# The entry to a backward attention loop, and three smaller edits, in a transformer block's training step

## The chip, the cores and the metric

One core of a Trainium2 chip. The time is device microseconds for one execution, the median of several; a profiled execution of the same kernel gives the trace. The engines are TensorE (PE; its weight loads PEld), VectorE (DVE), ScalarE (ACT), GpSimd (POOL) and SyncE (SP, which here only issues DMAs). DMAs are issued from SP's queue, and in the backward loop from ScalarE's too.

## The reference

A transformer block with adaptive layer norm, and its gradient. `x` is 2048 x 512 in bf16; attention has 32 heads of 16; the dense part has 1792 hidden units with a squared ReLU.

```python
mod = (silu(c) @ w_mod).reshape(...)              # sa, ca, ga, sb, cb, gb
h = layernorm(x) * (1 + ca) + sa
x = x + ga * attention(h, wqkv, wo)               # 32 heads, softmax over 2048 keys
h = layernorm(x) * (1 + cb) + sb
x = x + gb * (relu(h @ w1 + b1) ** 2 @ w2 + b2)
out, vjp = jax.vjp(f, x, wqkv, wo, w1, b1, w2, b2, c, w_mod);  grads = vjp(grad_out)
```

The outputs are the block's output and the gradients of all nine arguments.

## The kernel before

**Stages.** First a preparation (layer norm, q, k, v; L130 to L282). Then the forward attention (L625 to L653): 512 units, each a chunk of 512 queries (`qc`, 4), a group of 4 heads (`hg`, 8) and a tile of 128 keys (`kt`, 16). A unit makes scores (`fscore`), takes exps on ScalarE, and two units later multiplies by V (`fpv`). V carries a column of ones, so that row 16 of each head's result is the softmax denominator.

After the last key tile of a head group, VectorE copies the accumulator to `ostage` (L576), GpSimd casts it to `obf` (L578), SP copies four denominators to `rrows` (L581) and transposes `obf` into `O_un` (L582). After the last group of a chunk, `ffinish` (L586) transposes the denominators on TensorE (L591), inverts them and makes `O_c`. It runs when the loop has come to a unit number noted at L584, or in the loop's last pass. It also starts `dense_chunk` for those 512 tokens: a Python generator that the loop advances by one step per unit, 105 steps for chunks 0 to 2 with the pauses that it asks for. A dense chunk covers the output projection, the second layer norm, the up-projection (from `h2T`), its gradient, the down-projection and the gradient of the attention output (`attn_grad`, L495). The fourth dense chunk runs after the attention loop, in a tail (L743 to L755), interleaved with the weight gradients `dwa`; in it `act` is true, and some evictions go to ScalarE.

**The second layer norm's affine.** `xn2_c` is transposed by a DMA into `h2T` (L378), and four VectorE operations apply scale and shift per feature (L380), each over 128 partitions x 512. GpSimd makes the token-major `h2_c` at the same time (L383, L384).

**The entry to the backward loop (L772 to L956).** Two sets of tiles, `hsets`, hold k, v, q and dO of four heads at a time, each 128 x 2048 in bf16, with 16 rows of every 32 used and the rest filled with ones (k, v) or zeros (q, dO). GpSimd fills both sets first (L778). SP then loads set 0: `iqs` (token-major q), four DMAs each for k and q, the maxima `m_st` into a row of q, four for v (L792). Then follow `dOs_tok` (2 MB, one DMA, L797), `KS_tok` (2 MB, L800), the four loads of dO and one of its row `d_st` (L949, issued at L123), and `wT_pad` (2 MB of padded transposed weights, L956), which is read only in the last stage. GpSimd also fills a padding of KS_tok (L799) and two tiles `qz` (L803), and writes scaled q into `qz` (L850).

**The backward loop (L957 to L977).** 512 units again, four to a block, sixteen blocks to a head group. Step `j` is half a unit; a unit makes scores (L872), exps (L874), dP (L884) and dS on VectorE (L886). SP transposes dS by DMA, 512 KB per unit, into `dsT` (L892). TensorE adds to dK and dV (L900, L909), and, in steps 6 and 7 of the next block, to dQ from `dsT` and `KS_tok` (L927). `dsT` has two buffers, `dS_u` four.

**What sets the order.** In the forward loop the order of TensorE and ScalarE is as written, by `manual_schedule`; that of VectorE, GpSimd and SP comes from a planner that takes instructions as they become ready, by program order. In the backward loop the order of all but GpSimd is as written. A queue runs in order: a DMA that waits holds back those behind it. In the loop, DMAs for later heads are put at steps with `at(j, ...)`; `load` issues on ScalarE's queue. Loads of the next head begin at step 14 of each head (128 steps); stores of dK/dV and dQ go out at its end.

Of the kernel before, what the change touches and what calls it, by code (L numbers as in the profile page):

```python
# [14 lines left out]
AF = mybir.ActivationFunctionType  # L15
# [9 lines left out]
DH = 16  # L25
# [9 lines left out]
def kernel(  # L35
# [6 lines left out]
    n = A_x.shape[1]  # L42
    assert A_x.shape[2] == D and n % 512 == 0 and n <= 2048
    TT = n // P
    QC = n // 512
# [8 lines left out]
    DVE = nc.vector  # L54
    ACT = nc.scalar
    POOL = nc.gpsimd
    SP = nc.sync
# [13 lines left out]
    modcol = persist.tile([P, 6, DC], F32, name="modcol")  # L71
# [12 lines left out]
    dOs_st = dram.tile([P, TT, D], BF, name="dOs_st")  # L84
# [7 lines left out]
    dOT_st = dram.tile([D, n], BF, name="dOT_st")  # L92
    m_st = dram.tile([H, n], BF, name="m_st")
    d_st = dram.tile([H, n], BF, name="d_st")
    wpad_st = dram.tile([D, 16 * P], BF, name="wpad_st")
    wT_st = dram.tile([16, P, D], BF, name="wT_st")
# [17 lines left out]
    def row_loads(dst, srcT, hg, cols, aux=None):  # L114
        for h in range(4):
            i = hg * 4 + h
            yield dst[32 * h:32 * h + DH, :], srcT[i * DH:(i + 1) * DH, cols]
        if aux is not None:
            yield dst.rearrange("(h c) n -> c h n", h=4)[DH], aux[hg * 4:(hg + 1) * 4, cols]

    def load_rows(*args):
        for to, fro in row_loads(*args):
            SP.dma_start(out=to, in_=fro)  # L123
# [160 lines left out]
    with ExitStack() as ph:  # L284
# [16 lines left out]
        def flat(x):  # L301
            return x.rearrange("p a b -> p (a b)")
# [30 lines left out]
        def dense_chunk(c, O_c, act):  # L333
# [40 lines left out]
            for ti in range(4):  # L374
                t = 4 * c + ti
                DVE.tensor_scalar(xn2_c[:, ti, :], x1_c[:, ti, :], mv4[:, ti, 0:1], rstd2[:, t:t + 1], ALU.subtract, ALU.mult)
            h2T = cb.tile([P, 4, DC, P], BF, name="h2T", tag="T4")
            SP.dma_start(out=h2T.rearrange("p t o q -> p (t o) q"), in_=flat(xn2_c), transpose=True)  # L378
            for ic in range(DC):
                DVE.tensor_scalar(h2T[:, :, ic, :], h2T[:, :, ic, :],  # L380
                                  modcol[:, 4, ic:ic + 1], modcol[:, 3, ic:ic + 1], ALU.mult, ALU.add)
            h2_c = cb.tile([P, 4, D], BF, name="h2_c", tag="h2")
# [52 lines left out]
            for ti in range(4):  # L435
                t = 4 * c + ti
# [101 lines left out]
        fh, fe, fcur, fdone, dense = {}, {}, {}, [], []  # L538
# [21 lines left out]
        def fpv(u):  # L560
            qc, hg, kt = funits[u]
            if kt == 0:
                fcur["o"] = pools["o"].tile([P, 512], F32, name="oacc", tag="oacc")
                if hg == 0:
                    fcur["rr"] = ework.tile([H, 512], F32, name="rrows", tag="rrows", bufs=1)
                    fcur["ou"] = ework.tile([P, 4, HG, P], BF, name="O_un", tag="O_un", bufs=1)
            oacc = fcur["o"]
            ET = fe.pop(u)
            for hq in range(4):
                h = hg * 4 + hq  # L570
                lhsT = vaug[:, kt].rearrange("p h c -> p (h c)")[:, h * (DH + 1):h * (DH + 1) + 32]
                PE.matmul(oacc[32 * hq:32 * hq + 32, :], lhsT, ET[:, hq, :],  # L572
                          start=(kt == 0), stop=(kt == TT - 1), tile_position=(0, 32 * hq), skip_group_check=True)
            if kt == TT - 1:
                ostage = ework.tile([P, 512], F32, name="ostage", tag="ostage", bufs=1)
                DVE.tensor_copy(ostage[:], oacc[:])  # L576
                obf = ework.tile([P, 512], BF, name="obf", tag="obf", bufs=2)
                POOL.tensor_copy(obf[:], ostage[:])  # L578
                for hq in range(4):
                    h = hg * 4 + hq  # L580
                    SP.dma_start(out=fcur["rr"][h:h + 1, :], in_=ostage[32 * hq + 16:32 * hq + 17, :])  # L581
                SP.dma_start(out=fcur["ou"][:, :, hg, :], in_=obf[:], transpose=True)  # L582
                if hg == HG - 1:
                    fdone.append((u + 5, qc, fcur["rr"], fcur["ou"]))  # L584

        def ffinish(qc, rr, ou):  # L586
            O_c = cb.tile([P, 4, D], BF, name="O_c", tag="O_c")
            for ti in range(4):
                t = qc * 4 + ti
                pr = mm()  # L590
                PE.transpose(pr[:, 0:H], rr[0:H, ti * P:(ti + 1) * P], identf[0:H, 0:H])  # L591
                DVE.reciprocal(r_inv[:, t, :], pr[:, 0:H])
                DVE.tensor_tensor(O_c[:, ti, :].rearrange("p (g h d) -> p g h d", g=HG, h=4),
                                  ou[:, ti].rearrange("p g (h c) -> p g h c", h=4)[:, :, :, 0:DH],
                                  r_inv[:, t, :].rearrange("p (g h) -> p g h", g=HG).unsqueeze(3).to_broadcast([P, HG, 4, DH]),
                                  ALU.mult)
            SP.dma_start(out=o_st[:, qc * 4:(qc + 1) * 4, :], in_=O_c[:])
            dense.append(dense_chunk(qc, O_c, qc == QC - 1))
# [32 lines left out]
        with ExitStack() as ph2:  # L631
            pools["s"] = ph2.enter_context(tc.tile_pool(name="psS", bufs=3, space=bass.MemoryType.PSUM))
            pools["o"] = ph2.enter_context(tc.tile_pool(name="psO", bufs=1, space=bass.MemoryType.PSUM))
            pools["mm"] = ph2.enter_context(tc.tile_pool(name="psM", bufs=1, space=bass.MemoryType.PSUM))
            with tc.manual_schedule(engines={PE.engine, ACT.engine}):
                for u in range(NF + 6):
                    if u < NF:
                        if funits[u][2] == 4 and u + TT < NF:
                            fload(*funits[u + TT][0:2])
                        fscore(u)  # L640
                    if 2 <= u < NF + 2:
                        fpv(u - 2)
                    if u % 4 == 2 and u // 4 < 16:
                        later_stage(u // 4)
                    if dense and wait == 0:
                        wait = next(dense[0], -1)
                        if wait < 0:
                            dense.pop(0)
                            wait = 0
                    elif wait > 0:  # L650
                        wait -= 1
                    if not open_group[0] and fdone and (u - 2 >= fdone[0][0] or u == NF + 5):
                        ffinish(*fdone.pop(0)[1:])  # L653
# [118 lines left out]
    strm, hsets = [], []  # L772

    def head_set(i):
        strm.append(tc.alloc_tile_pool(name=f"phIs{i}", bufs=1, side="right"))
        hs = {key: strm[i].tile([P, n], BF, name=f"i{key}{i}") for key in ("k", "v", "q", "do")}
        for key in hs:
            POOL.memset(hs[key][:], 1.0 if key in ("k", "v") else 0.0)  # L778
        hs["qs"] = strm[i].tile([P, TT, 64], BF, name=f"iqs{i}")
        hsets.append(hs)  # L780

    def kvq_loads(hg):
        hs = hsets[hg % 2]
        yield hs["qs"][:], q_st[hg]
        yield from row_loads(hs["k"], qkT_st[1], hg, slice(0, n))
        yield from row_loads(hs["q"], qkT_st[0], hg, slice(0, n), m_st)
        yield from row_loads(hs["v"], vT_st, hg, slice(0, n))

    for i in range(2):
        head_set(i)  # L790
    for to, fro in kvq_loads(0):
        SP.dma_start(out=to, in_=fro)  # L792
    jpool = tc.alloc_tile_pool(name="jpool", bufs=1)
    wT_pad = jpool.tile([P, 16, D], BF, name="wT_pad")
    qpool = tc.alloc_tile_pool(name="qpool", bufs=1)
    dOs_tok = qpool.tile([P, TT, D], BF, name="dOs_tok")
    SP.dma_start(out=dOs_tok[:], in_=dOs_st[:])  # L797
    KS_tok = qpool.tile([P, TT, QPAD], BF, name="KS_tok")
    POOL.memset(KS_tok[:, :, D:QPAD], 0.0)  # L799
    SP.dma_start(out=KS_tok[:, :, 0:D], in_=k_st[:])  # L800
    qz = [qpool.tile([P, TT, 4, 32], BF, name=f"qz{i}") for i in range(2)]
    for i in range(2):
        POOL.memset(qz[i][:], 0.0)  # L803

# [10 lines left out]
    with ExitStack() as ph:  # L817
# [21 lines left out]
        def at(j, f, *args):  # L839
            todo.setdefault(j, []).append((f, args))  # L840
# [6 lines left out]

        def spread_qz(hg):
            st = hsets[hg % 2]
            POOL.tensor_scalar(qz[hg % 2][:, :, :, DH:2 * DH], st["qs"].rearrange("p t (h d) -> p t h d", h=4),  # L850
                               SCALE, None, ALU.mult)

        def plan_head(hg):
# [92 lines left out]
                    else:  # L946
                        at(cur["j"] + 6, load, dQtP[hg], st["dq"][:])

        load_rows(hsets[0]["do"], dOT_st, 0, slice(0, n), d_st)  # L949
        spread_qz(0)  # L950
        load_head(0)
        for hg in range(1, HG):
            plan_head(hg)
        for i, key in enumerate(("q", "k", "v", "do")):
            at((HG - 1) * 128 + 14 + 8 * i, load_grads, i // 2, (hsets[0]["q"], hsets[0]["k"]) if i < 2 else (hsets[0]["v"], hsets[0]["do"]), i % 2)
        SP.dma_start(out=wT_pad[:], in_=wT_st.rearrange("j p d -> p j d"))  # L956
        with tc.manual_schedule(engines={PE.engine, ACT.engine, DVE.engine, SP.engine}):  # L957
            for j in range(2 * NU + 10):
                u, pair, sub = j // 2, j % 2, j % 8
# [202 lines left out]
    if _rest_zero:  # L1162
        zt = persist.tile([P, 2048], BF, name="zeros2048")
        DVE.memset(zt[:], 0.0)
        for o in _rest_zero:
# [9 lines left out]
            while r0 < R:  # L1175
                rr = min(P, R - r0)
# [36 lines left out]
```

## Time and profile before

| | us |
|---|---|
| median of 3 runs | 2971.3 (2969.22 to 2974.01) |
| profiled execution | 2962.25 |
| its span | 2960.5 |
| forward attention loop, about | 186 to 1103 of the span |
| tail with the fourth dense chunk | 1103 to 1322 |
| entry to the backward loop (first fill to first dP matmul) | 1322.1 to 1347.6 |
| backward loop, first to last dQ eviction | 1367.9 to 2782.5 |

| engine | busy us | share |
|---|---|---|
| PE | 2502.8 | 85% |
| PEld | 728.6 | 25% |
| DVE | 1712.2 | 58% |
| ACT | 2185.0 | 74% |
| POOL | 444.1 | 15% |

The shares are means over stages with different limits, so a change is judged in its own stretch. The profile's queue names mean DMA issues (SPq, ACTq); a name such as `dsT<-dS_u` is destination and source. The granted TensorE clock has a mean of 0.80 of full speed.

### The profile page before, as it was taken

What the parts mean: (1) busy time and instruction counts of PE and PEld (TensorE: products, weight loads), DVE (VectorE), ACT (ScalarE), POOL (GpSimd) and SP (SyncE); (2) the same over time, 40 slices, a digit from 0 to 9 for tenths busy, and PEclk for the clock granted to TensorE, in tenths of its full rate; (3) what the DMA queues carried; (4) which work ended last, traced back from release to release, by engine and by line L of the source; (5) the groups of instructions that cost most, each with busy time, mean ns of one, the idle gap of its engine ahead of it and who ended that gap; (6) DMA issues with size and microseconds to landing.
All of it is one profiled execution on the core that took longest, in us unless ns stands there. A gap on an engine that the chain in (4) does not pass through costs nothing.

```text
span 2960.5 us, 45854 instructions
## 1 busy us (share of the span) xinstructions
PE 2502.8 (85%) x16942; PEld 728.6 (25%) x17006; DVE 1712.2 (58%) x2046; ACT 2185.0 (74%) x3432; POOL 444.1 (15%) x385
## 2 busy tenths in 40 slices
PE   6799988878888886987888888889898888888878
PEld 2111122212212222431222222222222222222323
DVE  6100044233413424526888888888888888878783
ACT  4699999989989981006777777778777777878521
POOL 3010012020311221211110101101010110101261
PEclk9555578768957878996889898888778888879989
DMA  9751144326344446739999999999999999999941
GB/s 254 199 131 41 28 104 118 93 69 140 96 103 105 134 111 174 163 107 237 198 208 200 197 209 199 208 196 205 202 199 208 203 205 198 202 209 201 202 117 43
DMA packets 1395889, 474.98 MB, mean 160 GB/s; under 512 B 1320321, under 2 KB 1369989, under 8 KB 1395281
## 3 DMA queue, kind: packets, MB, share of 16 engines
q1 hardware_dynamic: 1389088, 455.82, 78.1%
q10 hardware_dynamic: 6576, 16.23, 1.6%
q8 instruction: 134, 2.20, 0.3%
q14 instruction: 91, 0.74, 0.1%
HBM read 83.78 MB, written 61.10 MB: 49 GB/s over the span
## 4 chain that ended last, share of the span: by engine, by line
PE 27%; DMA 17%; ACT 7%; DVE 5%; issue 3%; SPq 1%; POOL 1%; DVEq 0%; ACTq 0%; POOLq 0%
DMA dsT<-dS_u 15%; PE psS_u L872 8%; ACT E_u L874 6%; PE dqacc L927 5%; PE accVK L909 4%; PE accVK L900 3%; DVE dS_u L886 2%; PE psS_x L872 2%; PE dwa L724 2%; PE psD_u L884 1%; PE pwq L1129 1%; PE dwa L733 1%; DMA out_dram<-dwres 1%; DVE prod L1106 0%; SPq L1023 0%
## 5 line engine op out<-in xcount | busy, mean ns | idle before, releaser
L886 DVE TENSOR_TENSOR dS_u<-psD_u,E_u 128x1024 bf16<-128x1024 f32 x1024 | 1190.9, 1217 | 258.3 <-PE psD_u L884 178.7
L874 ACT ACTIVATE E_u<-psS_u 128x512 bf16<-128x512 f32 x1536 | 866.0, 632 | 283.6 <-PE psD_u L884 256.2
L558 ACT ACTIVATE ET<-psST 128x1024 bf16<-128x1024 f32 x1024 | 947.1, 1235 | 40.9 <-PE psST L556 40.5
L872 PE MATMUL psS_u<-ik,iq 32*128 32x512 bf16 x1536 | 523.4, 438 | 20.7 <-DMA iq<-m_st 11.6
L556 PE MATMUL psST<-qt_sb,kt_sb 32*128 32x512 bf16 x2048 | 460.9, 508 | 87.3 <-ACT ET L558 36.7
L884 PE MATMUL psD_u<-iv,ido 32*128 32x512 bf16 x2048 | 453.6, 437 | 29.3 <-DMA ido<-d_st 13.1
L927 PE MATMUL dqacc<-dsT,KS_tok 128*32 128x512 bf16 x2048 | 212.7, 502 | 150.2 <-DMA dsT<-dS_u 113.5
L874 ACT ACTIVATE E_u<-psS_x 128x512 bf16<-128x512 f32 x512 | 332.5, 649 | 6.1 <-PE psD_u L884 4.4
L572 PE MATMUL oacc<-ET,vaug 128*32 128x512 bf16 x2048 | 271.5, 520 | 4.7 <-DVE ostage L576 4.1
L576 DVE COPY ostage<-oacc 128x512 f32<-128x512 f32 x32 | 22.0, 689 | 377.1 <-PE oacc L572 348.3
L900 PE MATMUL accVK<-dS_u,qz 128*32 128x512 bf16 x2048 | 228.0, 434 | 13.8 <-ACT vkb L912 13.0
L909 PE MATMUL accVK<-E_u,dOs_tok 128*16 128x512 bf16 x2048 | 228.8, 437 | 0.0
L942 POOL TENSOR_TENSOR dQacc<-dQacc,dqtmp 128x512 f32<-128x512 f32 x64 | 81.2, 1269 | 913.2 <-ACT dqtmp L937 913.2
L872 PE MATMUL psS_x<-ik,iq 32*128 32x512 bf16 x512 | 214.3, 419 | 0.6
L556 PEld LDWEIGHTS <-kt_sb 32*128 32x128 bf16 x2048 | 89.9, 96 | 461.1 <-issue 455.0
L872 PEld LDWEIGHTS <-iq 32*128 32x128 bf16 x2048 | 99.7, 93 | 375.9 <-issue 362.9
L884 PEld LDWEIGHTS <-ido 32*128 32x128 bf16 x2048 | 123.1, 93 | 230.9 <-issue 207.8
L736 ACT ACTIVATE dwres<-dwa 128x512 bf16<-128x512 f32 (+1 forms) x17 | 9.7, 572 | 140.8 <-PE dwa L733 71.8
L927 PEld LDWEIGHTS <-KS_tok 128*32 128x32 bf16 x2048 | 52.7, 106 | 210.3 <-issue 165.4
L572 PEld LDWEIGHTS <-vaug 128*32 128x32 bf16 x2048 | 56.0, 98 | 184.3 <-issue 184.3
L900 PEld LDWEIGHTS <-qz 128*32 128x32 bf16 x2048 | 56.1, 94 | 154.1 <-issue 153.8
L578 POOL CAST obf<-ostage 128x512 bf16<-128x512 f32 x32 | 20.6, 644 | 448.6 <-DVE ostage L576 428.8
(244 smaller groups left out, 2051.3 us busy)
## 6 DMA issues: line engine op xcount, KB each, us to landing
kt_sb<-qkT_st SPq DMA_DIRECT2D x128, 64.0 KB
dsT<-dS_u SPq DMA_TRANSPOSE x512
wA<-in_B_w_dram SPq DMA_DIRECT2D x4, 1792.0 KB
wB<-in_B_w_dram SPq DMA_DIRECT2D x4, 1792.0 KB
s_st<-tk SPq DMA_DIRECT2D x9, 512.0 KB
dz_st<-tk SPq DMA_DIRECT2D x9, 512.0 KB
slab<-s_st SPq DMA_DIRECT2D x9, 512.0 KB
slab<-dz_st SPq DMA_DIRECT2D x9, 512.0 KB
```

Source lines behind the costliest of these rows:

```text
L556: PE.matmul(ps[:, hi, :], kt_sb[r:r + 32, kt * P:(kt + 1) * P], qt_sb[r:r + 32, :], start=True, stop=True, tile_position=(r, 0))
L558: ACT.activation(ET[:, 2 * pair:2 * pair + 2, :], ps[:], AF.Exp, scale=SCALE)
L572: PE.matmul(oacc[32 * hq:32 * hq + 32, :], lhsT, ET[:, hq, :], start=(kt == 0), stop=(kt == TT - 1), tile_position=(0, 32 * hq), skip_grou ...
L724: PE.matmul(acc[:, 0:w], lhsT, rhs, start=(t == 0), stop=False)
L872: PE.matmul(psS[:], st["q"][r:r + 32, qt * P:(qt + 1) * P], st["k"][r:r + 32, kc * 512:kc * 512 + 512], start=True, stop=True, tile_positi ...
L874: ACT.activation(bst[u][0][:, hq, :], psS[:], AF.Exp, scale=SCALE)
L884: PE.matmul(psD[:, hi, :], st["do"][r:r + 32, qt * P:(qt + 1) * P], st["v"][r:r + 32, kc * 512:kc * 512 + 512], start=True, stop=True, til ...
L886: DVE.tensor_tensor(dS_u[:, 2 * pair:2 * pair + 2, :], psD[:], E_u[:, 2 * pair:2 * pair + 2, :], ALU.mult)
L900: PE.matmul(cur["vk"][32 * hq:32 * hq + 32, :], hst[hg]["qz"][:, qt, hq, :], bst[u][1][:, hq, :], start=(qt == 0), stop=False, tile_positi ...
L909: PE.matmul(acc[32 * hq:32 * hq + DH, :], dOs_tok[:, qt, (hg * 4 + hq) * DH:(hg * 4 + hq + 1) * DH], E_u[:, hq, :], start=False, stop=(qt ...
L927: PE.matmul(acc[32 * hq:32 * hq + 32, :], KS_tok[:, kc * 4 + kt, h * DH:h * DH + 32], tT[:, :, hq * 4 + kt, :], start=(kt == 0), stop=(kt ...
L942: POOL.tensor_tensor(dst2, dst, tmp[:], ALU.add)
```

## The change

There are five edits.

1. A forward chunk ends ten units after its last accumulation is evicted instead of five (`fdone`).
2. In the fourth dense chunk, ScalarE applies the affine to feature tiles 0 and 2 of h2T, VectorE to 1 and 3.
3. At the entry, VectorE fills tile set 0 and `qz[0]` and writes the first scaled q; GpSimd keeps set 1 (now filled last), the padding and `qz[1]`.
4. SP loads dO right after k, q and v; `dOs_tok` comes in four DMAs behind it.
5. The load of `wT_pad` leaves the entry and is issued from ScalarE's queue at step 400 of the loop's 1034.

```diff
             for ic in range(DC):
+                if act and ic % 2 == 0:
+                    ACT.activation(h2T[:, :, ic, :], h2T[:, :, ic, :], AF.Identity,
+                                   bias=modcol[:, 3, ic:ic + 1], scale=modcol[:, 4, ic:ic + 1])
+                    continue
                 DVE.tensor_scalar(h2T[:, :, ic, :], h2T[:, :, ic, :],
...
-                    fdone.append((u + 5, qc, fcur["rr"], fcur["ou"]))
+                    fdone.append((u + 10, qc, fcur["rr"], fcur["ou"]))
...
-            POOL.memset(hs[key][:], 1.0 if key in ("k", "v") else 0.0)
+            (DVE if i == 0 else POOL).memset(hs[key][:], 1.0 if key in ("k", "v") else 0.0)
...
-    for i in range(2):
-        head_set(i)
+    head_set(0)
     for to, fro in kvq_loads(0):
         SP.dma_start(out=to, in_=fro)
+    load_rows(hsets[0]["do"], dOT_st, 0, slice(0, n), d_st)
...
-    SP.dma_start(out=dOs_tok[:], in_=dOs_st[:])
+    for g in range(QC):
+        SP.dma_start(out=dOs_tok[:, 4 * g:4 * g + 4, :], in_=dOs_st[:, 4 * g:4 * g + 4, :])
...
-    for i in range(2):
-        POOL.memset(qz[i][:], 0.0)
+    DVE.memset(qz[0][:], 0.0)
+    POOL.memset(qz[1][:], 0.0)
+    head_set(1)
...
-            POOL.tensor_scalar(qz[hg % 2][:, :, :, DH:2 * DH], st["qs"].rearrange("p t (h d) -> p t h d", h=4),
+            (DVE if hg == 0 else POOL).tensor_scalar(qz[hg % 2][:, :, :, DH:2 * DH], st["qs"].rearrange("p t (h d) -> p t h d", h=4),
                                SCALE, None, ALU.mult)
...
-        load_rows(hsets[0]["do"], dOT_st, 0, slice(0, n), d_st)
         spread_qz(0)
...
-        SP.dma_start(out=wT_pad[:], in_=wT_st.rearrange("j p d -> p j d"))
+        at(400, load, wT_pad[:], wT_st.rearrange("j p d -> p j d"))
```

## The prediction

> **What bounds the kernel now.** The page's 40 slices come first: ScalarE at 9 or 8 tenths in the forward attention (slices 3 to 15), the DMA engines at 9 throughout the backward loop (slices 19 to 38). The change touches the ends of forward chunks, one step of the tail between the two loops, the entry to the backward loop, and the middle of that loop. Each needs its own stretch of the trace.
>
> Forward chunk ends, from the timeline (start us, length us, engine, line, operation, and in brackets the idle time ahead of it with what ended it):
>
> ```profile
> 356.21 1.02 ACT L558 ACTIVATE ET<-psST 128x1024 bf16<-128x1024 f32 x1 [1.98 <-PE psST L556]
> ...
> 598.61 0.34 SPq L348 DMA_DIRECT2D gf_st<-gf_c  x1
> ...
> 604.38 2.46 SPq L581 DMA_DIRECT2D rrows<-ostage  x4
> ...
> 608.06 0.28 PE L591 MATMUL pm<-identf,rrows 32*128 32x32 f32 x1 [5.44 <-DMA rrows<-ostage]
> ...
> 612.33 1.94 ACT L558 ACTIVATE ET<-psST 128x1024 bf16<-128x1024 f32 x2 [8.18 <-PE psST L556]
> ...
> 863.64 0.28 PE L591 MATMUL pm<-identf,rrows 32*128 32x32 f32 x1 [5.71 <-DMA rrows<-ostage]
> ...
> 868.07 2.85 ACT L558 ACTIVATE ET<-psST 128x1024 bf16<-128x1024 f32 x3 [8.59 <-PE psST L556]
> ```
>
> TensorE's order is written out by hand, so while the transposes of L591 wait for the denominators `rrows`, no scores are made and ScalarE starves. At the first chunk end the rows are there in time (1.98 us of ScalarE idle). At the second and third, SP is caught ahead of them in the `gf_st` store of the next dense chunk, which waits 8.2 us for GpSimd's gf_c.
>
> The entry, from the chain of waits:
>
> ```profile
> 1322.50 1.10 DMA rows_st<-racc
> ...
> 1334.38 1.75 POOL ido L778
> 1336.13 0.25 POOL KS_tok L799
> 1336.38 1.76 POOL qz L803
> 1338.14 1.35 SPq L123
> ...
> 1340.92 6.62 DMA ido<-d_st
> ...
> 1347.63 0.62 PE psD_u L884 x4
> ```
>
> The dO loads leave SP at 1338 to 1341 and the first dP matmul starts at 1347.63, though q and k were there at 1331.34. Beside it, DMA by half microseconds: the 4.2 MB of dOs_tok and KS_tok flow from 1333.75 to about 1344.7 (10.95 us, some 383 GB/s), dO until 1347.5, wT_pad (2.1 MB) from 1346.5 to 1352.3 (5.8 us). The first block's transposes get the DMA only then; its last one is issued at 1358.58 and the first dQ matmul goes at 1364.89: 12.4 us after the bulk has gone. So this entry ends with DMA work, not with the dP matmul. This reading decides the size of the gain.
>
> The loop, from the waits of TensorE between 1400 and 2700 us (total, times, longest):
>
> ```profile
> PE dqacc L927 <- DMA dsT<-dS_u: 109.2, 65, 5.8
> ```
>
> and from windows around the end of the third head (busy us per engine, granted clock, DMA share, GB/s):
>
> ```profile
> 1886.00:1896.00 10.00, 9.37 (x87) 2.96 (x84) 9.03 (x9) 9.72 (x20) 1.27 (x1) 1.00 1.14 220
> 1896.00:1902.00 6.00, 1.10 (x12) 0.28 (x12) 2.06 (x2) 0.00 (x0) 1.30 (x1) 0.55 1.10 265
> 1902.00:1916.00 14.00, 13.73 (x104) 2.93 (x100) 10.77 (x9) 10.87 (x21) 1.47 (x1) 0.50 1.14 193
> ```
>
> About half the blocks of four units wait for their transposes. DMA moves some 204 GB/s all the time, at which four transposes (2.1 MB) take 10.3 of a block's 11.1 us. Where a head ends, 1 MB of stores and a 256 KB load join in: all engines but DMA stop, and by the starts of the dQ evictions that block takes 15.5 to 16.1 us instead of 11 (mid heads). So 1.25 MB more DMA costs 4.5 us, with 0.5 us regained in the next block.
>
> **What the Trainium skill says.** "DMA: Bandwidth & Descriptors", section "Issuing engines are not separate DMA queues": DMAs issued by different engines run on the same 16 engines and interleave. The trace agrees: ScalarE's stores at a head's end hold back SP's transposes (5.37 us of TensorE idle at 1900.90). "VectorE: DVE Perf Modes", "Zero memsets can be issued as uint32": a memset takes a cycle per element whatever the type; a zero fill can be halved. The trace has VectorE fills of 165 ns for 128 bf16 and 70 ns for 14 f32, hence 0.83 ns per element and an estimated 1.76 us for 2048; that page's cycle at 0.96 GHz would give 2.13 us. "SBUF — State Buffer", "Who interferes with whom": VectorE in its two-port modes and GpSimd lock each other out. It fits h2T: 1.22 us each in the tail beside GpSimd's 4 us h2_c, where xn_c in the same shape takes 0.41.
>
> **The parts.** Baseline is the profiled execution: span 2960.5, time 2962.25.
>
> *Chunk end at u+10.* The two row copies before and at that chunk end lie 30.4 us apart for 16 units, so five units are 9.5 us, and the finish moves from 602.6 (608.06 less the 5.44 waited) to 612.1; rows landing at 608 would be in time. What is left is the first chunk's 1.98 us: (8.18 - 1.98) + (8.59 - 1.98) = 12.8 us. ScalarE is busy 875 of the 917 us between 186 and 1103, so its idle time is the forward's time. The whole dense chunk moves with it: 105 steps from unit 13 of the next chunk end at 118 of 128, so there is room. Its g_c load (589.28) moves behind the copies of the row (data ready at 594.25), so the `gf_st` wait should no longer block them. -12.8 us; between 0, if SP's backlog moves along, and -14. The last chunk finishes where it did (the loop's last pass), but GpSimd's 4.06 us gf_c, now 1091.68, slides to about 1102 and before the last obf cast (1103.74): +1.5, between 0 and +4.
>
> *h2T shared.* Four VectorE operations of 1.22 us stand between the transpose and the up-projection (4.64 us from 1144.75). Two go to ScalarE, where the row of that shape (xn, 128x512 from SBUF) takes 0.806 us: 1.6 beside VectorE's 2.4. ScalarE has nothing else there (12.06 us idle before 1150.46). -2.1, or 0 at the worst.
>
> *Entry.* Fills of set 0 on VectorE start behind its last row copy (1322.5), not at 1322.09: at 1.76 us the q fill ends at 1327.8, against 1327.39 now. VectorE's fills are thus no faster; set 1, KS padding and qz1 only leave the line. SP then issues at 0.42 us each: q and m to 1330.1, v to 1332.1, dO to 1333.8, d 1334.3, dOs_tok in four 1335.9, KS_tok 1336.5. d lands 2 us later, the first dP goes at about 1336.5: 11 us earlier. But the bulk starts flowing at 1336.5 instead of 1333.75 and, with wT_pad out of the way, ends at 1336.5 + 10.95 = 1347.4 instead of 1352.3. The transposes sit behind it in SP's queue (KS_tok is needed anyway): first dQ matmul at 1347.4 + 12.4 = 1359.8 instead of 1364.9. **-5 us**, between -2 (fills of 2.13 us and a slow dOs_tok in pieces) and -9 (zero fills halved, transposes overlapping). qz0's fill and scaling on VectorE, bounded by twice 0.41 and 2.8 us, are done by about 1334 to 1336, before K's first use at 1340; without that cover at most 2 us.
>
> *wT_pad at step 400.* 2.1 MB in a stretch bound by DMA, two steps after a head end. Alone it took 5.8 us; the head-end rate (4.5 per 1.25 MB) would make 7.5. The block at 1904 to 1916 has some 1.5 us of empty DMA to give. I take +5, between +1.5 and +9. Issue on ScalarE's queue is 0.4 us. If that queue backs up, the k load of step 403 and all exps behind it wait, as SP's dO load stood 6.6 us behind 4 MB; they would mostly stand in the same stall.
>
> Sum: -12.8 + 1.5 - 2.1 - 5 + 5 = **-13.4 us**, 2948.9 in the profiled execution. The median of the runs is 2971.3, 9 us above that execution, so 2957.9; I say 2958.
>
> **Rivals.** *A (0.56)* is the above, 2951 to 2965 on its own. *B (0.17):* the forward stall moves along. For: SP's order is planned from program order and readiness, and the backlog is made by the dense chunk, which shifts by the same five units. Against: g_c falls behind the row copies. Then -0.6: about 2971. *C (0.15):* the loop has cover for wT_pad (1.5 of it paid) and the entry gains 6: -12.8 + 1.5 - 2.1 - 6 + 1.5 = -17.9, 2953. For: half the blocks don't wait for transposes. Against: the head ends. *D (0.12), slower:* at both inner chunk ends SP keeps its order, with the next head's q rows behind the dense chunk's dOT, delta and row stores. Now that row load is issued at 588.67 and already costs TensorE 1.8 us at 590.51; 10 us later it stalls the scores 10 us at each of two ends, +20: 2978. It decides from about 7 us per end upward (13.4 / 2). Against: in the new program order the load (unit 244) comes before the last of those stores (245), where before it came after.
>
> **How the numbers follow.** 0.2% is 5.9 us, about what measurement can tell. Faster (below 2965.4): 0.49 of A, 0.15 of C, 0.02 of B. Same: 0.06 of A, 0.13 of B, 0.04 of D. Slower: 0.11, mostly D. The range runs from C with the entry's best value, 2946, over B with noise to 2976, just short of D.
>
> **What would show it.** Right: no `rrows` wait at L591 in the second and third chunk end and ScalarE idle of about 2 us there; first dP near 1347.6 - 11 and first dQ only 5 us earlier, each after subtracting what the forward gave; DMA full from the bulk through the first block; one block near step 400 longer by some 5 us. Wrong: waits of psST for `qt_sb` at chunk starts (D), the `rrows` wait still there (B), or a first dQ earlier by 9 us or more, which would say that DMA was not what the entry ended with.

## The result, and the profile after

The kernel became slower. The kernel after takes 2981.66 us (median of 4 runs, 2979.35 to 2990.39), the kernel before 2970.27 (4 runs, 2969.22 to 2974.01) in the same comparison: a ratio of 1.0041, 95% interval 1.0019 to 1.0064. I had predicted 2958.0, with a range of 2946 to 2976. The profiled execution of after has a span of 2978.4 us, 17.9 more than the one of before.

A table of moments on the time axis shows where the difference arises. Each is the start of one instruction, in us from the start of the span.

| moment | before | after | difference |
|---|---|---|---|
| last accumulator of the second chunk copied | 593.6 | 592.2 | -1.4 |
| of the third chunk | 848.9 | 844.5 | -4.4 |
| of the last chunk | 1103.0 | 1095.6 | -7.4 |
| transpose of the last denominators (L591, L595 after) | 1110.6 | 1116.9 | +6.3 |
| first affine of h2T in the tail | 1144.8 | 1152.4 | +7.6 |
| first `racc` copy, ahead of the entry | 1320.0 | 1329.2 | +9.2 |
| first dP matmul | 1347.6 | 1345.6 | -2.0 |
| first dQ eviction | 1367.9 | 1372.4 | +4.5 |
| last dQ eviction | 2782.5 | 2798.4 | +15.9 |
| end of the span | 2960.5 | 2978.4 | +17.9 |

The forward loop did gain (7.4 us of the 12.8 that I had summed), and then lost it and more in one wait at its end. The entry gained 4.7 from the `racc` copies to the first dQ, and the loop lost 11.4.

The forward chunk ends, from the timeline of after (start us, length us, engine, line, operation, in brackets the idle time ahead of it and what ended it):

```profile
602.65 2.45 SPq L585 DMA_DIRECT2D rrows<-ostage  x4
604.83 4.06 POOL L346 TENSOR_TENSOR gf_c<-g_c,modbc 128x2048 bf16<-128x2048 bf16 x1
608.85 3.61 POOL L308 TENSOR_TENSOR racc<-racc,g_c 128x512 f32<-128x512 f32 x3
612.41 0.61 POOL L582 CAST obf<-ostage 128x512 bf16<-128x512 f32 x1
613.05 1.27 SPq L586 DMA_TRANSPOSE O_un<-obf  x1
616.62 0.31 PE L595 MATMUL pm<-identf,rrows 32*128 32x32 f32 x1 [5.20 <-DVE r_inv L596]
618.45 7.44 ACT L562 ACTIVATE ET<-psST 128x1024 bf16<-128x1024 f32 x8 [6.49 <-PE psST L560]
...
871.06 7.44 ACT L562 ACTIVATE ET<-psST 128x1024 bf16<-128x1024 f32 x8 [6.83 <-PE psST L560]
...
1080.30 3.83 SPq L521 DMA_TRANSPOSE dOT<-dOs_c  x3
...
1090.58 6.33 SPq L323 DMA_TRANSPOSE wB<-in_B_w_dram  x5
1096.96 0.58 SPq L338 DMA_DIRECT2D g_c<-in_grad_out_dram  x1
1102.46 4.05 POOL L346 TENSOR_TENSOR gf_c<-g_c,modbc 128x2048 bf16<-128x2048 bf16 x1
1106.54 2.06 SPq L350 DMA_TRANSPOSE gfT<-gf_c  x1
1109.62 2.84 SPq L585 DMA_DIRECT2D rrows<-ostage  x4
1110.02 0.61 POOL L582 CAST obf<-ostage 128x512 bf16<-128x512 f32 x1
1116.88 0.28 PE L595 MATMUL pm<-identf,rrows 32*128 32x32 f32 x1 [21.37 <-DMA rrows<-ostage]
```

Read it in two parts. At the second and third chunk end the denominators now come in time (`rrows` at 602.65), as predicted. But the third of the second end's four transposes waits 5.20 us for VectorE's `r_inv`. VectorE is in order, and ahead of it stands the first piece of `O_c`, which waits for `O_un`, whose cast to `obf` stands on GpSimd behind gf_c and three `racc` adds until 612.41, though its data were copied by about 592.9. ScalarE's idle time falls from 8.18 and 8.59 us to 6.49 and 6.83, not to 2.

At the last end SP has the transpose of gf_c ahead of the last four denominators. It was so in before too, as its timeline shows:

```profile
1085.96 0.58 SPq L338 DMA_DIRECT2D g_c<-in_grad_out_dram  x1
...
1091.68 4.06 POOL L346 TENSOR_TENSOR gf_c<-g_c,modbc 128x2048 bf16<-128x2048 bf16 x1
...
1098.34 2.03 SPq L350 DMA_TRANSPOSE gfT<-gf_c  x1
...
1103.70 2.58 SPq L581 DMA_DIRECT2D rrows<-ostage  x4
...
1110.60 0.28 PE L591 MATMUL pm<-identf,rrows 32*128 32x32 f32 x1 [7.71 <-DMA O_un<-obf]
```

There, gf_c was ready at 1095.7, some 7 us before the last accumulator was copied (1103.0), so the transpose was out of the way. In after, SP's order is another one. In before, g_c left at 1085.96, and behind it came the last `dOT` transpose of the third dense chunk, the stores of that chunk's attention gradient, and the denominators and `O_un` of the seventh head group. In after all of these stand ahead of g_c, some 10 us of issues, with the last five transposes of w1 behind them. The third dense chunk itself comes only 1.5 us later on the time axis (its first `dOT` transpose starts at 1070.59 against 1069.12), since the loop is ahead by most of what five units take.

So g_c leaves SP at 1096.96, and gf_c is ready only at 1106.5. SP issues nothing between 1098.1 and 1106.54: it waits for gf_c with the transpose `gfT`, and the denominators, ready since about 1096.3, stand behind it and leave at 1109.62. The wait grows from 7.71 to 21.37 us.

The entry, from the chain of waits of after (start, length, what):

```profile
1331.72 1.11 DMA rows_st<-racc
...
1334.21 0.56 DVE iv L782
...
1336.14 0.92 DVE iq L782
...
1343.25 2.25 DMA ido<-d_st
...
1345.59 0.62 PE psD_u L890 x4
...
1348.69 10.86 DMA dsT<-dS_u
```

The fills are 1.76 us for ones and 0.91 for zeros, dO follows v at once, and the dP matmuls wait for nothing else. The last line is the first transpose of dS, which stands behind the bulk of the loads; the next dS waits for it until 1359.6, and the first dQ matmul follows at 1369.4.

The loop, from the waits of TensorE between 1400 and 2700 us (total, times, longest), and from windows around the end of the third head (busy us of PE, PEld, DVE, ACT and POOL, granted clock, DMA share, GB/s):

```profile
PE dqacc L933 <- DMA dsT<-dS_u: 114.2, 65, 7.4
```

```profile
1897.00:1904.00 7.00, 6.79 (x56) 2.08 (x52) 6.27 (x7) 7.00 (x15) 1.27 (x1) 1.00 1.16 214
1904.00:1916.00 12.00, 7.09 (x56) 1.60 (x56) 6.88 (x6) 5.36 (x11) 2.77 (x1) 0.57 1.05 218
1916.00:1926.00 10.00, 3.22 (x28) 0.90 (x24) 4.80 (x5) 3.88 (x8) 0.00 (x0) 0.78 1.17 274
```

The third window is the new one: TensorE has 3.2 us of work in ten, and the longest wait for `dsT`, 7.4 us, ends at 1926.6. This block, from the 49th dQ eviction to the next, took 17.8 us where before took 11.5. I call it block 49.

### The profile page after: what moved, and what is told of

Same layout as the page of the kernel before. It is cut to its first block, busy times and chain, and to the rows that moved or that the text cites. A ratio compares the mean times of both kernels' runs of the same rounds, so it can differ in the third digit from the quotient of the medians.

```text
span 2978.4 us, 45926 instructions
## 1 busy us (share of the span) xinstructions
PE 2510.4 (84%) x17006; PEld 729.0 (24%) x17006; DVE 1722.6 (58%) x2050; ACT 2184.4 (73%) x3434; POOL 433.1 (15%) x379
## 4 chain that ended last, share of the span: by engine, by line
PE 23%; DMA 17%; ACT 6%; DVE 5%; issue 3%; POOL 0%; SPq 0%; ACTq 0%; DVEq 0%; POOLq 0%
DMA dsT<-dS_u 16%; PE psS_u L878 7%; ACT E_u L880 6%; PE dqacc L933 5%; PE accVK L915 3%; PE accVK L906 3%; DVE dS_u L892 2%; PE psS_x L878 2%; PE pwq L1134 1%; PE psD_u L890 1%; DVE prod L1111 1%; DVE c12a L1119 0%; ACT vkb L918 0%; DVE tqa L1121 0%; DVE dxn L1108 0%
## 5 line engine op out<-in xcount | busy, mean ns | idle before, releaser
L429 DVE SCALAR_TENSOR_TENSOR rT<-pm,rT 128x512 bf16<-128x512 f32 x56 | 38.7, 692 | 114.2 <-PE pm L426 114.2
```

The costliest lines, as they stand in the source:

```text
L429: DVE.scalar_tensor_tensor(out=dzT[:, fc, :], in0=pds[:], scalar=2.0, in1=rT[:, fc, :], op0=ALU.mult, op1=ALU.mult, accum_out=db1p[:])
```

## The experiments with the kernel's own data movement

Theory Q says that the loss comes from the order of SP's queue at the end of the forward loop. Theory W says that the load of `wT_pad` in the loop costs some 6 us. The first four kernels ran as one group with the kernel before (2968.02 us there, 41 runs). Ratios are to before.

**Chunk ends back at u+5, everything else as in after.**

```diff
-                    fdone.append((u + 10, qc, fcur["rr"], fcur["ou"]))
+                    fdone.append((u + 5, qc, fcur["rr"], fcur["ou"]))
```

> The changed kernel with only the chunk end put back to five units; edits 2 to 5 stay. Theory Q (the loss sits at the end of the forward loop, where the last denominators stand behind the transpose of gf_c in SP's queue): the last chunk's first L591-type transpose comes 6 us earlier than in the changed kernel, its wait shrinks from 21.4 to about 8 us, and the time falls by about 6 us to 2975, still 4 to 5 above before. Theory W (the loss is the wT_pad load in a loop bound by DMA, with what follows from it): the time stays at 2979 to 2982.

2971.27 us (13 runs), ratio 1.0009 (0.9999 to 1.0018). The timeline of this kernel at the last end:

```profile
1110.25 0.28 PE L595 MATMUL pm<-identf,rrows 32*128 32x32 f32 x1 [8.12 <-DMA O_un<-obf]
```

The wait is back at 8.12 us, at the moment where before has it, and SP issues g_c at 1085.37 again, in before's order. So the edit of `fdone` makes the wait, and most of the loss. Block 49 is 6.8 us longer, against 4.2 gained at the entry in this profile. Without `u + 10` the other edits come to +3.3 us, which the interval doesn't tell from nothing.

**The edit of the chunk ends alone, in the kernel before.**

```diff
-                    fdone.append((u + 5, qc, fcur["rr"], fcur["ou"]))
+                    fdone.append((u + 10, qc, fcur["rr"], fcur["ou"]))
```

> The kernel before with only the chunk end at ten units. Theory Q: the inner chunk ends give 7.4 us, the last end takes 13.7, so about +6: 2976, with a wait of about 21 us for rrows ahead of the last chunk's transposes. Theory W: the forward's gain is all there is, -7 us: 2963.

2973.37 us (21 runs), ratio 1.0018 (1.0009 to 1.0026). From its timeline:

```profile
1118.26 0.28 PE L591 MATMUL pm<-identf,rrows 32*128 32x32 f32 x1 [21.78 <-DMA rrows<-ostage]
```

The same wait, in a kernel that has nothing else of the change, and the same late g_c (1098.10): 6.4 us ahead at the last accumulator, 7.7 behind at this transpose. The edit that I valued at -11.3 is worth about +5 by itself.

**u+10 at the first two chunk ends, u+5 at the third.**

```diff
-                    fdone.append((u + 10, qc, fcur["rr"], fcur["ou"]))
+                    fdone.append((u + (10 if qc < QC - 2 else 5), qc, fcur["rr"], fcur["ou"]))
```

> The changed kernel, but the chunk end at ten units only for the first two chunks and at five for the third, so that the third dense chunk is not late at the end of the forward loop. Theory Q: the inner gain of about 7 us stays and the last wait is back at about 8 us: 13 us less than the changed kernel, 2968, 2 us faster than before. Theory W: 2979 to 2982 as the changed kernel.

2975.86 us (13 runs), ratio 1.0028 (1.0018 to 1.0037), where theory Q expected 2968: a miss. The last wait did go back (8.01 us), but the third end became worse than in either kernel. Its timeline there:

```profile
858.75 4.04 POOL L346 TENSOR_TENSOR gf_c<-g_c,modbc 128x2048 bf16<-128x2048 bf16 x1
...
861.53 0.28 PE L595 MATMUL pm<-identf,rrows 32*128 32x32 f32 x1 [7.26 <-DMA rrows<-ostage]
...
866.30 0.61 POOL L582 CAST obf<-ostage 128x512 bf16<-128x512 f32 x1
...
870.54 0.31 PE L595 MATMUL pm<-identf,rrows 32*128 32x32 f32 x1 [7.97 <-DVE r_inv L596]
...
872.38 14.77 ACT L562 ACTIVATE ET<-psST 128x1024 bf16<-128x1024 f32 x16 [16.56 <-PE psST L560]
```

The finish came five units earlier, while the dense chunk ahead of it kept its later place, and SP issued g_c only at 853.40. So both the denominators (7.26) and the cast behind gf_c (7.97) were late, and ScalarE idled 16.56 us. The chunk end and the queues of SP and GpSimd have to fit each other; a shift of one alone moves the stall.

**`wT_pad` at the entry again, on SP behind `KS_tok`.**

```diff
-        at(400, load, wT_pad[:], wT_st.rearrange("j p d -> p j d"))
+        SP.dma_start(out=wT_pad[:], in_=wT_st.rearrange("j p d -> p j d"))
```

> The changed kernel with wT_pad loaded at the entry again, behind KS_tok on SP's queue. If the entry ends with DMA work, as the prediction read it: the block near step 400 loses its 6 us, but the first dQ eviction comes about 6 us later, so the time moves by less than 2 us: 2980 to 2983; the first dP stays 11 us earlier than before. Rival, that the entry ends with the first dP: the entry keeps its gain and the time falls by 6 us or more, to 2976 or less. Theory W: 2970 to 2976.

2981.18 us (5 runs), ratio 1.0049 (1.0036 to 1.0061), the same as after. Against the `racc` copies the first dP is 11.3 us earlier than in before, and the first dQ 1.1 later, where after has it 4.7 earlier. The load costs 5.8 us at the entry and 6.3 in the loop. Both readings hold: the entry ends with DMA work, and moving the load saves nothing.

## The experiments with plain DMAs

If Q is right, the u+10 edit is not bad in itself. It fails because what stands ahead of the last denominators comes late. To test this I made SP's queue quicker. In the following kernels each DMA transpose is a plain DMA of as many bytes, so the data behind it are not transposed and other values are computed; order and sizes of the rest stay. For the weights the same bytes come from the other matrix:

```diff
-                    SP.dma_start(out=w[:, fc, :], in_=B_w1[:, fc * P:(fc + 1) * P], transpose=True)
+                    plain(SP, w[:, fc, :], B_w2[fc * P:(fc + 1) * P, :])
...
-            SP.dma_start(out=gfT.rearrange("p t o q -> p (t o) q"), in_=flat(gf_c), transpose=True)
+            plain(SP, gfT.rearrange("p t o q -> p (t o) q"), flat(gf_c))
```

I compare within a group of runs only: the tail between the loops was about 5 us longer in the second and third group than in the first, in kernels whose tail is alike.

**First group: before, after, after with g_c first, after with u+5.** In the third, the load of g_c (with `g_c = cb.tile(...)`) is written ahead of the weight loads:

```diff
-            w1_nat = load_wA(False)
-            w1T = load_wB(True)
             g_c = cb.tile([P, 4, D], BF, name="g_c", tag="g_c")
             SP.dma_start(out=g_c[:], in_=g_dram[:, ts, :])
+            w1_nat = load_wA(False)
+            w1T = load_wB(True)
```

> The kernel before with each of its DMA transposes written as a plain DMA of as many bytes, so that the data behind them are not transposed. It is the base for three kernels changed in the same way. A plain issue takes SP about 0.4 us where a transpose takes 1.25, so SP's backlog at chunk ends should be smaller than in before: waits for the denominators at the second and third chunk end below 5 us. In the backward loop DMA should have room, so TensorE should hardly wait for dsT. Theory Q: at the last end the order (gfT's copy ahead of the last denominators) is as in before, with g_c issued early enough: last wait of the transposes at or below 8 us, ended by O_un or the rows.

> The kernel after with its DMA transposes written as plain DMAs in the same way. Theory Q: g_c stands behind eight copies of w1 issued late (0.4 us each, not behind fourteen transposes of 1.25), gf_c of 4 us on GpSimd follows, and the last denominators wait behind gfT's copy: last wait 3 to 7 us longer than in the plain form of before, ended by rrows. Theory W (the step-400 load costs what DMA's lack of room makes it cost): the block there is longer by less than 2 us, not by 6.3. Rival to W: 5 to 6 us all the same, from ScalarE's queue or the head's end. In sum this kernel lies within 8 us of the plain form of before on either side.

> The plain form of after with the load of g_c written ahead of the weight loads at the start of the dense chunk (SP then issues it behind two of the w1 copies). Theory Q: gf_c no longer comes late, the last wait falls by 3 to 7 us back to that of the plain form of before, and the inner chunk ends get 1 to 2 us shorter since the cast to obf no longer stands behind gf_c: 5 to 10 us below the plain form of after. Rival R (the last rows wait for something else, such as the w1 copies themselves or the last cast): last wait as in the plain form of after, time within 2 us of it.

> The plain form of after with chunk ends at u+5: the entry, the shared affine and the moved load alone, with DMA that has room. Theory W: the entry's gain is left and the step-400 load is nearly free: first dQ eviction 4 to 9 us earlier against the racc copies than in the plain form of before, and 3 to 8 us below it in all. Rival: the same time as the plain form of before within 2 us.

| plain form of | median us (4 runs each) | last wait of the transposes | block 49 |
|---|---|---|---|
| before | 2670.24 | 7.41 | 9.0 |
| after | 2660.27 | 8.11 | 14.0 |
| after, g_c first | 2661.54 | 7.66 | 15.0 |
| after, u+5 | 2668.78 | 7.57 | 15.0 |

Here the same change is 10 us faster than before, and 8.5 of it come from u+10, the edit that cost 5 or more in the kernel with its transposes. The timeline of the plain form of after at the last end shows why:

```profile
1075.90 4.06 POOL L353 TENSOR_TENSOR gf_c<-g_c,modbc 128x2048 bf16<-128x2048 bf16 x1
...
1079.99 0.48 SPq L38 DMA_DIRECT2D gfT<-gf_c  x1
...
1081.42 2.60 SPq L592 DMA_DIRECT2D rrows<-ostage  x4
...
1088.72 0.28 PE L602 MATMUL pm<-identf,rrows 32*128 32x32 f32 x1 [8.11 <-DMA rrows<-ostage]
```

gf_c's copy is gone at 1080.5 and the last accumulator was copied at 1080.7. It is in time by less than a microsecond, so my expectation of a wait 3 to 7 us longer was wrong, and g_c first had nothing left to give at this end (5 to 10 us were expected of it in all). It does free the cast to `obf` at the inner ends: the times between accumulator copies fall there from 32.3 and 32.9 us to 31.4 and 31.4, but the median doesn't move.

The other surprise is block 49. DMA has room in these kernels (in the loop of before's plain form its share is 0.64, and TensorE waits for `dsT` 0.9 us in all), and yet the load costs 5 to 6 us. Theory W's reason, that the load costs what DMA's lack of room makes it cost, doesn't hold here. With u+5 the load takes back most of what the entry gains (8.1 us from the `racc` copies to the first dQ): 1.5 us are left of the 3 to 8 expected. The timeline of the plain form with u+5 names another cause:

```profile
1766.77 0.38 ACTq L859 DMA_DIRECT2D wT_pad<-wT_st  x1
...
1769.71 5.67 ACTq L859 DMA_DIRECT2D ik<-qkT_st  x1
...
1775.48 0.60 ACT L887 ACTIVATE E_u<-psS_x 128x512 bf16<-128x512 f32 x1 [4.77 <-issue]
```

In that kernel the load of k three steps later takes ScalarE's queue 5.67 us to issue instead of 0.33, and the exps stand behind it. In the plain form of after that issue took 2.51 us, and TensorE waited 1.96 us for `dsT` besides. In after itself the issue took 0.86 us, and it was TensorE's wait for `dsT` that grew. The same 2 MB cost about the same, by another way in each.

**Second group: gf_c delayed, and `wT_pad` in pieces.** In three kernels GpSimd computes gf_c of the last chunk three times over. The order of SP's queue stays (in the plain form of after only the copy for `gfs` falls behind the denominators).

```diff
-            POOL.tensor_tensor(gf_c[:], g_c[:], gb_bc.unsqueeze(1).to_broadcast([P, 4, D]), ALU.mult)
+            for _ in range(3 if act else 1):
+                POOL.tensor_tensor(gf_c[:], g_c[:], gb_bc.unsqueeze(1).to_broadcast([P, 4, D]), ALU.mult)
```

> The plain form of before with GpSimd's gf_c of the last dense chunk computed three times over (4.06 us more twice: 8.1 us of delay put into one link of the suspected chain, with the order of SP's queue unchanged). In the plain form of before gf_c ended at 1077.2 and the last accumulator was copied at 1087.9, 10.7 us later. Theory Q (the last denominators wait in SP's queue behind gfT's copy, and so behind gf_c): the 10.7 us take up the 8.1, the last wait stays at about 7.5 to 8 us and the time at 2670, within 3 us. Rival R (the last wait has nothing to do with gf_c): no change here either; it is the next kernel that tells them apart.

> The plain form of after with gf_c of the last dense chunk computed three times over in the same way. In the plain form of after gf_c ended at 1080.0, and the last accumulator was copied at 1080.7. Theory Q: gf_c ends at about 1088.1, the denominators leave SP at about 1089 instead of 1081.4, the last wait grows from 8.1 to about 15.5 us, ended by rrows, and the time rises by some 7 us to about 2667, so that most of what u+10 gained is gone. Rival R: last wait 8 us, time 2660.

> The plain form of after with g_c loaded first, and gf_c of the last dense chunk computed three times over. gf_c ended at 1058.2 in the kernel without the repetition, 22 us ahead of the last accumulator. Theory Q: the 8.1 us vanish in the 22, last wait about 7.7 us, time 2661 within 3 us, 6 or 7 below the plain form of after with the same repetition: the order of g_c is then a remedy. Rival: the load on GpSimd itself costs time wherever it stands: about 2668.

In the plain form of after:

```profile
1087.11 4.05 POOL L354 TENSOR_TENSOR gf_c<-g_c,modbc 128x2048 bf16<-128x2048 bf16 x1
...
1091.18 0.49 SPq L38 DMA_DIRECT2D gfT<-gf_c  x1
1091.77 2.59 SPq L593 DMA_DIRECT2D rrows<-ostage  x4
...
1095.61 0.28 PE L603 MATMUL pm<-identf,rrows 32*128 32x32 f32 x1 [13.94 <-DMA rrows<-ostage]
```

And in the plain form with g_c first:

```profile
1067.60 4.05 POOL L354 TENSOR_TENSOR gf_c<-g_c,modbc 128x2048 bf16<-128x2048 bf16 x1
...
1082.96 2.50 SPq L593 DMA_DIRECT2D rrows<-ostage  x4
...
1090.27 0.28 PE L603 MATMUL pm<-identf,rrows 32*128 32x32 f32 x1 [8.11 <-DMA rrows<-ostage]
```

With the delay in gf_c, the denominators leave 0.6 us after gf_c's end and the wait is 13.94 us; 2679.64 us. With the same delay and g_c first, it is 8.11 us; 2667.46 (4 and 5 runs). That is 12.2 us between two kernels that differ only in where g_c is loaded: 5.3 at this transpose, 9.1 at the `racc` copies; what adds the difference was not followed. Both times lie above the expected 2667 and 2661, by 12.6 and 6.5 us, of which the longer tail of this group makes some 5. In the plain form of before the delay changes the wait to 8.51 only; its 2675.15 are nearer to the expected 2670 than they look, since its transpose of the denominators is where it was (1095.3, against 1095.2 in the first group) and the tail is 5.1 us longer, as in the other kernels of this group. So theory Q holds in the plain forms: gf_c ahead of the last denominators makes the wait when it is late, and an earlier g_c removes it.

The fourth kernel loads `wT_pad` in four pieces of 512 KB:

```diff
-        at(400, load, wT_pad[:], wT_st.rearrange("j p d -> p j d"))
+        for i in range(4):
+            at(425 + 20 * i, load, wT_pad[:, 4 * i:4 * i + 4, :], wT_st.rearrange("j p d -> p j d")[:, 4 * i:4 * i + 4, :])
```

> The plain form of after with wT_pad loaded in four pieces of 512 KB at steps 425, 445, 465 and 485 instead of one of 2 MB at step 400. In the plain form of after block 49 took 14.0 us instead of 9.0, and in the plain form with u+5 15.0: the load of k issued three steps behind the 2 MB held ScalarE's queue for 5.67 us. Theory L (the cost is one long transfer ahead of a short one in the same queue, not a lack of DMA room): no block from 49 to 64 stands out by over 1 us, four issues cost ScalarE 1.4 us, and the time is 4 to 5 us below the plain form of after: about 2655.5. Theory W as it stood (2 MB cost what they take from DMA, wherever they go): the cost is spread over the four blocks and the time stays at 2660.

Block 49 takes 9.0 us, but the median, 2661.87, doesn't show it against 2660.27 in the first group. So base and pieces ran once more together.

**Third group: before, after, after in pieces, and both remedies.**

> The plain form of before once more, as base on the chip of the next three: 2670, or some 5 more on a chip like that of the second group. Every theory: the plain form of after some 10 us below it.

> The plain form of after once more, on the same chip: 10 us below the base. Block 49 again at 14 to 15 us.

> The plain form of after with wT_pad in four pieces, on the same chip. Theory L (one long transfer ahead of a short one in ScalarE's queue is what costs): 4 to 5 us below the plain form of after. Theory W as it stood: same time within 1.5 us.

> Both remedies in the plain form of after: g_c loaded first and wT_pad in four pieces. If the two add up: 1 us from g_c (the last wait has little left to give in the plain form) and 4 to 5 from the pieces, so 5 to 6 us below the plain form of after and about 15 below the plain form of before. If they don't: the same as the split alone.

| plain form of | median us | range (runs) | block 49 |
|---|---|---|---|
| before | 2673.45 | 2670.17 to 2681.83 (4) | 9.1 |
| after | 2667.12 | 2662.24 to 2669.88 (5) | 14.0 |
| after in pieces | 2661.42 | 2657.92 to 2665.04 (4) | 9.0 |
| both remedies | 2660.12 | 2657.34 to 2663.91 (4) | 9.1 |

The change is 6.3 us faster than before in this group (expected 10), the pieces save 5.7 more, where theory L (one long load ahead of a short one in the same queue is what costs) expected 4 to 5, and g_c first adds 1.3 that the ranges don't separate. The runs of after and of the pieces overlap in part; the block itself, 14.0 against 9.0, doesn't depend on that. Nor does the cost come back elsewhere in the loop: from first to last dQ eviction it takes 1158.4 us in the plain form of after, 1153.3 in pieces and 1151.6 in the plain form of before.

The pieces differ from the whole load in place too: they are issued 25 to 85 steps later, among the loads of q, v and dO. A whole load at such a place was not measured, so what size and place each contribute isn't shown.

What was not measured in the kernel with its transposes: g_c first, the pieces, the cast to `obf` on VectorE, and the entry's edits alone. There DMA has no room, so the pieces may be worth less; and that g_c first would turn the 21 us wait back is inferred from the plain forms.

## Why the prediction was wrong

**Chunk end, inner ends (-12.8).** The denominators were in time, and the `rrows` waits at the second and third end are gone. The gain is 7.4. The step that failed is what comes late next: I looked at SP alone. GpSimd's queue holds the cast to `obf` behind gf_c and `racc`, and at u+10 that falls on the chunk end (5.20 and 5.54 us of new waits). It did so in before too: at the second end the cast started at 602.10, 8 us after its data, but the denominators left SP later still, at 604.38, and hid it. In the plain forms g_c first frees the cast, and the inner ends become as short as the first (31.4 us).

**"Its g_c load moves behind the copies of the row."** It didn't. At the inner ends SP issues g_c (599.38) before the denominators (602.65); only the store of gf_c fell behind them. This reading of the order was also my argument against rival B. B's sign, an `rrows` wait still at the inner ends, did not come. But its thought, that the stall moves along with the dense chunk, is nearer to the trace than mine: at the inner ends a stall came back in part, by way of GpSimd, and at the last end, which B did not name, it cost more than all of the gain.

**The last end (+1.5, between 0 and +4).** This is the step that cost most: it measured +13.7 (from -7.4 at the last accumulator to +6.3 at the transpose), and with +1.5 in its place the medians would be about equal. I had gf_c's new place right as a number (about 1102 predicted, 1102.46 measured), in part by luck: I had only the dense chunk's delay for it, and it was SP's new order that put g_c back. And I followed gf_c only to the cast on its own engine. Its reader gfT stands ahead of the last denominators in SP's queue; before's timeline shows that order, and I did not look at it. The repetition of gf_c in the plain forms shows this link.

**h2T (-2.1).** It gave nothing. ScalarE's two take 1.52 us together, as said, but the 1.22 us each for VectorE's were a mean over unlike ones. In before the first of the four takes 3.67 us and the other three 0.40 each, and the up-projection starts behind the first, not behind all four. From the timelines of before and of after:

```profile
1144.23 4.04 POOL L384 TENSOR_TENSOR h_c<-h_c,modbc 128x2048 bf16<-128x2048 bf16 x1
1144.75 3.67 DVE L380 TENSOR_SCALAR h2T<-h2T,modcol 128x512 bf16<-128x512 bf16 x1 [4.72 <-issue]
1148.48 1.04 PE L405 MATMUL pm<-h2T,wA 128*128 128x512 bf16 x2 [11.30 <-DVE h2T L380]
```

```profile
1151.26 4.05 POOL L388 TENSOR_TENSOR h_c<-h_c,modbc 128x2048 bf16<-128x2048 bf16 x1
1152.36 3.10 DVE L384 TENSOR_SCALAR h2T<-h2T,modcol 128x512 bf16<-128x512 bf16 x1 [5.30 <-issue]
1155.51 1.01 PE L409 MATMUL pm<-h2T,wA 128*128 128x512 bf16 x2 [1.76 <-DVE h2T L384]
```

In both, VectorE's first operation ends 0.15 us after GpSimd's second one on `h2_c`. That is the lock-out which the prediction names, but it holds one operation for as long as GpSimd runs and doesn't slow all four, so half as many are not half as long. GpSimd starts on `h2_c` when `xn2_c` is ready. From then to the up-projection (in after to all but its first matmul, which ScalarE's tile lets go early) it is 8.46 us in before and 8.46 in after; in the six kernels with transposes it is 8.45 or 8.46, with ScalarE's share or without.

The tail as a whole is 2.9 longer from the transpose to the `racc` copies. It goes with u+10 (212.2 us with that edit alone, 210.5 in after with u+5, against 209.4 and 212.4 in before and after); I found no one cause for it.

**Entry (-5).** Right, in both numbers: first dP 11.3 us earlier (11 predicted), first dQ 4.7, so "this entry ends with DMA work, not with the dP matmul" stands, as the fourth kernel confirms. Two small errors in the fills cancel: q's fill takes 0.91 us and not 1.76, but the fills start up to 0.4 us late. And the 12.4 us from the end of the bulk to the first dQ are 12.6 by the prediction's own moments (1352.3 and 1364.9).

**`wT_pad` (+5, between +1.5 and +9).** 6.3 measured. As a size it was right. As a reason, "a stretch bound by DMA" is only half: with DMA room it cost 5 to 6 as well, for the most part by the queue of ScalarE, which I named but expected to hide in the same stall.

**The rest.** The span of before's profiled execution was a quick one. From first to last dQ eviction it took 1414.6 us, and after 1425.9; without block 49 the difference is 5.1. Over the profiles of the six kernels with transposes this stretch, less what block 49 has too much, lies between 1412 and 1427, and it goes with how quick the profiled execution was: u+5, the quickest of its 13 runs, has 1412.1, the kernel with `wT_pad` at the entry, the slowest of its five, 1426.7. In the plain forms the loop less block 49 takes 1143.2 in before and 1143.6 in after. So I count these 5 us, and the last 2 to the end of the span, as scatter; that the entry's new order slows the loop beside DMA transposes is not excluded. In sum: -7.4 + 13.7 + 2.9 - 4.7 + 6.3 + 5.1 + 2.0 = 17.9 in the profiles; 11.4 in the medians.

Rival D did not come: in the forward loop TensorE waits for q rows once, for 1.9 us, where in before it did twice, 2.8 us in all.

## What to carry to other kernels

Before a step is moved later, read from the timeline what each in-order queue, DMA queues and GpSimd included, holds behind the work that moves with it, at the last pass of the loop as well as at the inner ones: here the same edit cost 13.7 us at the last pass. Measure its slack as the time from the late link to its reader's other inputs (here 7 us in before, none in after). Look at single operations before a mean over a few is halved: one long one can hide in it. And look at what stands behind a large load in its queue: here four pieces at later steps removed the 5 us that one of 2 MB cost.

## What the runs showed of the hardware that I had not expected

A VectorE operation waited out a whole GpSimd operation. In each of the 18 profiles one of VectorE's h2T operations in the tail took 3.1 to 4.2 us and ended 0.15 us after GpSimd's second operation on `h2_c`, where the shortest took 0.40.

Behind a 2 MB load on ScalarE's queue the next issue on that queue lasted 5.67 us in the plain form with u+5, 2.5 to 5.9 us in the six plain forms that load it whole, and ScalarE's activations waited with it. With four loads of 512 KB at later steps, the k, q, v and dO loads between them were issued in 0.31 to 0.33 us.

Replacing the DMA transposes by plain DMAs of the same bytes took 300 us from the kernel (2969.43 to 2670.24), 262 of them between the first and the last dQ eviction (1414.6 against 1152.3 us in the profiles). DMA moved some 202 GB/s in this loop with the transposes and had no room; with plain DMAs it moved 248 at a busy share of 0.64. The granted clock was 0.85 there with the transposes and 1.00 without, so how much of the 262 us is the transposes' rate alone isn't shown.

The VectorE fill of 2048 bf16 ones took 1.76 us, as the prediction had estimated from the trace, and not 2.13; that of zeros took 0.91, carried out as 1024 uint32.
